# Padding rows of the expert slots written once the counts are known, and the first tokens' transposes moved to other PSUM banks

## The chip, the cores and the metric

One core of one Trainium2 chip runs the whole program. The metric is device microseconds (us) from the start to the end of one execution, lower is better. The notation of the rows: PE is TensorE's matmuls, DVE is VectorE, ACT is ScalarE, POOL is GpSimd, SP is SyncE, which here issues most of the DMAs; a "q" behind an engine's name is its sequencer (SPq), and L151 is line 151 of the kernel before.

## The reference

An mLSTM attention feeds a mixture of experts, and this a three-way maximum layer. What matters here is the middle part: a token with a positive skip score goes to one of eight experts, the others pass through.

```python
def _moe_ref(x, w_skip, w_gate, w1, w2):
    do_compute = x @ w_skip > 0
    out = x.copy()
    xc = x[do_compute]
    logits = xc @ w_gate
    e_idx = np.argmax(logits, axis=1)
    ...
    for e in range(E):
        mask = e_idx == e
        h = np.maximum(xc[mask] @ w1[e], 0.0)
        y[mask] = gate_w[mask, None] * (h @ w2[e])
    out[do_compute] = xc + y
    return out

def _moe2_ref(x, w1, w2, w3, w_out):
    h = np.maximum(np.maximum(x @ w1, x @ w2), x @ w3)
    return h @ w_out
```

There are 3072 tokens of 320 numbers, 8 experts with a hidden size of 1024, and a hidden size of 768 in the last layer.

## The kernel before

**Stages.** `attention` runs over 24 tiles of 128 tokens (index i in its long loop). For each it loads TP, KP and small rows (SA, SM), scores (`score`, L900), weighs, and puts the tokens' output with their routing numbers into a row of 323 words, which an indirect DMA on GpSimd scatters into a table in DRAM (`scatter`, L1118). Beside it the weights of the last layer are loaded by ScalarE's queue (mraw, L210) and split into a high and a low half for float32r matmuls. The table has eight sections of slots, one for each expert, and behind them one row for every token by its place. A tile of an expert's tokens is 128 slots; slots behind the expert's last token must hold rows whose index lies out of range, so that what is computed from them is written nowhere. Such a row is `zrow` (its index words are set in `consts`). `pads` (L777, its DMA at L781) writes 256 of them into the first slots of one section, in iterations 0 to 7, before any token is scattered.

**The seam.** When all tokens are routed, `counted` (L352 and following) works out with small VectorE operations which expert stands at which place of the order, how many tokens each has, and some addresses, all in one integer tile `cnt_i`. The generator `experts` then runs up to its first `yield`: it reads the eight experts' numbers into SP's registers (`ids`, L145), issues the first two weights (`load`, L151), the first expert's x (`xload`, L456: tiles 0 and 1 as one DMA, then tile 2 by itself), and three weights more. The first expert in the order is the largest and may have three tiles; its third tile is not covered by `pads`, so `xload` reads an address from `cnt_i` into a register and writes 128 rows of `zrow` behind the tokens (L453, L454), and tile 2 is loaded after that.

During this, TensorE works on the first of the last layer's blocks of 512 tokens that need no expert (`mixed_block`, called by attention as `early["run"]`, driven by `fill`). Its six hidden blocks end with two pairs of output groups: the first pair in the banks "row" (ic and pv), the second in "tr" (mi and pl). Between the pairs stands `xprep(0, j)` for j = 0 and 1, the transposes of the first expert's x (`x_parts`, L278 and L279), also in "tr". ScalarE and VectorE evacuate these (xT, L280 to L283).

**The experts' weights.** There are 64 of them, 384 KB for a slab of the first layer, 320 KB for one of the second. A raw weight is loaded into one of five buffers (RAWS), then ScalarE casts it (L160) and VectorE or GpSimd makes the low half (L161); the split weights stand in a ring of twelve. `step` splits the next and issues one more load, in program order between the matmuls. The first expert's four first-layer slabs are split while attention's mixed block runs; its four second-layer slabs are weights 5 to 8. In a slab s, `l1` (L471, into bank pd) and `few1` (L404 and L410, into ps) are followed by two splits, so ScalarE's queue holds hH and r of the slab, sH of the slab before, and the two casts, in this order.

**Order and waits.** All engines run in order, and the program's order is the order of the calls. Accesses to the table are tracked as a whole where addresses come from registers; `Ctx.apart` tells the scheduler for which groups of DMAs no order is needed ("slots" for the scatters, "xl" for the loads of x, "y" for the results, "pad" and "last" for the third tile). The DMAs of SP and ACT signal their landing on eight semaphores (DMAHW0 to DMAHW7), which are handed round, so a DMA also waits for the one eight before it.

Of the kernel before, what the change touches and what calls it, by code (L numbers as in the profile page):

```python
# [12 lines left out]
I32 = mybir.dt.int32  # L13
AF = mybir.ActivationFunctionType
ALU = mybir.AluOpType
# [6 lines left out]
N = B * S  # L22
DM = H * D
E, FF = 8, 1024
F2 = 768
D1 = D + 1
CAP = N + 128
RW = DM + 3
# [4 lines left out]
ST = 256  # L33
# [6 lines left out]
TILES = (3, 2, 1, 2, 1, 2, 1, 2)  # L40
# [11 lines left out]
def bc(ap, shape):  # L52
    return ap.to_broadcast(shape)


def build(tc, tp, kp, og, gates, w9, w1, w2, m1, m2, out):
    nc = tc.nc
    with ExitStack() as top:
        top.enter_context(tc.manual_schedule())
        cp = top.enter_context(tc.tile_pool(name="const", bufs=1))  # L60
        dram = top.enter_context(tc.tile_pool(name="dram", bufs=1, space=bass.MemoryType.DRAM))
        table = dram.tile([ROWS, RW], F32, name="table")
        rows = dram.tile([NC, 3, 2, B * H, NB], BF16, name="rows")

        k = Ctx()
        k.tc, k.nc, k.cp, k.out = tc, nc, cp, out
        k.table, k.rows = table, rows
        k.psum = top.enter_context(tc.tile_pool(name="psum", bufs=1, space=PSUM))
        k.ident = cp.tile([128, 128], F32, name="ident")

        k.zrow = cp.tile([128, RW], F32, name="zrow")

        k.cnt_i = cp.tile([1, 3 * E + 3], I32, name="cnt_i")

        k.ordr = cp.tile([1, E], F32, name="ordr")
        k.caps = cp.tile([1, E], F32, name="caps")

        mp = Mixed(k, top, m1, m2)  # L80
        wts = Weights(k, w1, w2)
        with ExitStack() as left:
            moe = experts(k, wts, mp, left)
            attention(k, tp, kp, og, gates, w9, wts, left, mp, lambda: next(moe))
            next(moe, None)
            final(k, mp, wts)
        rare(k, mp, wts)
# [264 lines left out]
def counted(k):  # L352

    nc, cn, ci = k.nc, k.cn, k.cnt_i
    v = nc.vector
    f8 = k.cp.tile([1, 5, E], F32, name="f8")
    f88 = k.cp.tile([1, 2, E, E], F32, name="f88")
    m1 = k.cp.tile([1, 4], F32, name="m1")
    own, rank, ids, n = (f8[:, j] for j in range(4))
    em = k.em8[0:1, 0:E]  # L360
    across = lambda x: bc(x.unsqueeze(1), [1, E, E])
    down = lambda x: bc(x.unsqueeze(2), [1, E, E])

    v.scalar_tensor_tensor(own, cn[:, 0:E], float(E), em, ALU.mult, ALU.subtract)
    v.tensor_tensor(f88[:, 0], across(own), down(own), ALU.is_gt)
    v.tensor_reduce(rank, f88[:, 0], AX.X, ALU.add)
    v.tensor_scalar(rank, rank, float(-E), None, ALU.add)

    v.tensor_tensor(f88[:, 0], across(rank), down(k.ordr), ALU.is_equal)
    v.tensor_mul(f88[:, 1], f88[:, 0], across(em))  # L370
    v.tensor_reduce(ids, f88[:, 1], AX.X, ALU.add)
    v.tensor_scalar(ids, ids, float(E), None, ALU.add)
    v.tensor_copy(ci[:, 0:E], ids)
    v.tensor_mul(f88[:, 1], f88[:, 0], across(cn[:, 0:E]))
    v.tensor_reduce(n, f88[:, 1], AX.X, ALU.add)
    v.tensor_copy(ci[:, E : 2 * E], n)
    v.scalar_tensor_tensor(f8[:, 4], ids, float(CAP), n, ALU.mult, ALU.add)
    v.tensor_copy(ci[:, 2 * E : 3 * E], f8[:, 4])

    z = ORDER.index(0)  # L380
    v.tensor_scalar(m1[:, 0:1], n[:, z : z + 1], float(ST), None, ALU.max)
    v.scalar_tensor_tensor(m1[:, 0:1], ids[:, z : z + 1], float(CAP), m1[:, 0:1], ALU.mult, ALU.add)
    v.tensor_copy(ci[:, 3 * E : 3 * E + 1], m1[:, 0:1])

    v.tensor_sub(n, n, k.caps)
    v.tensor_reduce(m1[:, 1:2], n, AX.X, ALU.max)
    v.tensor_copy(ci[:, 3 * E + 1 : 3 * E + 2], m1[:, 1:2])

    v.tensor_scalar(m1[:, 2:3], cn[:, E : E + 1], -1.0, float(EARLY), ALU.mult, ALU.add)
    v.tensor_scalar(m1[:, 3:4], cn[:, E + 1 : E + 2], -1.0, float(T2), ALU.mult, ALU.add)  # L390
    v.tensor_max(m1[:, 2:3], m1[:, 2:3], m1[:, 3:4])

    v.tensor_max(m1[:, 2:3], m1[:, 2:3], m1[:, 1:2])
    v.tensor_scalar(m1[:, 2:3], m1[:, 2:3], 0.0, None, ALU.max)
    v.tensor_copy(ci[:, 3 * E + 2 : 3 * E + 3], m1[:, 2:3])


def few1(k, wts, p2, hp, e, s, xt):
# [18 lines left out]
def l2(k, wts, p2, e, hs, c, xrow, apart=True):  # L417

    nc = k.nc
# [9 lines left out]
    y = wts.y.tile([128, RW], F32, tag="y", name="y", bufs=3)  # L429
# [3 lines left out]
        k.table, bass.IndirectOffsetOnAxis(ap=xrow.bitcast(I32)[:, PLC : PLC + 1], axis=0), y, None,  # L433
        bounds_check=ROWS - 1, oob_is_err=False)
    if apart:
        k.apart(ins, "y", "y", "xl", "last", "pad")


def experts(k, wts, mp, left):
    tc, nc = k.tc, k.nc  # L440
    X, XT = {}, {}
    p2 = wts.x
    sp = [mybir.EngineType.SP]

    def xload(e):

        own = k.table[0 : E * CAP].rearrange("(e c) r -> e c r", c=CAP)[bass.ds(wts.at[e], 1)]
        X[e] = []
        for j, n in ((0, min(TILES[e], 2)), (2, 1))[0 : 1 + (TILES[e] > 2)]:
            t = p2.tile([128, n, RW], F32, tag="xb" if n > 1 else "xc", name="xb")  # L450
            rows = own[:, 128 * j : 128 * (j + n)].rearrange("o (j p) r -> p (o j) r", p=128)
            if j:
                free = nc.values_load(k.cnt_i[0:1, 3 * E : 3 * E + 1], engines=sp, min_val=0, max_val=E * CAP - 128)  # L453
                k.apart(nc.sync.dma_start(k.table[bass.ds(free, 128)], k.zrow), "pad", "y", "xl")  # L454

            k.apart(nc.sync.dma_start(t, rows), *(("last", "y") if j else ("xl", "y", "pad")))  # L456
            X[e] += [t[:, q] for q in range(n)]

    def xprep(e, j):

        if j % 2 == 0:
            n = 128 * min(TILES[e] - j, 2)
            XT[e, j // 2] = planes(*(p2.tile([128, a, n], F32R, tag=f"x{n}{a}", name="xT", bufs=1) for a in (3, 2)))
        x_parts(k, X[e][j], XT[e, j // 2], slice(128 * (j % 2), 128 * (j % 2) + 128))

    def l1(e, s, xt):

# [9 lines left out]

    counted(k)
    wts.ids(sp)
    wts.ahead(2)  # L480
    xload(0)
    wts.ahead(RAWS - 2)
    yield
    for j in range(2):
        xprep(0, j)
    yield
    own = ExitStack()
    wts.more(own)
# [90 lines left out]
def rare(k, mp, wts):  # L579


    tc, nc = k.tc, k.nc
    some = nc.values_load(k.cnt_i[0:1, 3 * E + 2 : 3 * E + 3], min_val=0, max_val=N)
    with tc.If(some > 0), ExitStack() as own:
        wts.open(own)
        wts.more(own)
# [39 lines left out]
            return wts.y.tile([128, RW], F32, tag="y", name="o", bufs=3)[:, 0:DM]  # L626

        hl = []
        left = nc.values_load(k.cnt_i[0:1, 3 * E + 1 : 3 * E + 2], min_val=-N, max_val=N)
        with tc.If(left > 0):  # L630
            for e in range(E):
                more(e)
# [8 lines left out]
def attention(k, tp, kp, og, gates, w9, wts, left, mp, moe):  # L641
    tc, nc = k.tc, k.nc
    rows, table, ident, zrow = k.rows, k.table, k.ident, k.zrow
    with ExitStack() as ctx:
# [128 lines left out]
        def w9split():  # L773
            nc.scalar.copy(w18[:, :, 0], w9s)
            nc.vector.tensor_sub(w18[:, :, 1], w9s, w18[:, :, 0].bitcast(F32))

        def pads(e):  # L777


            r0, n = e * CAP, ST  # L780
            nc.sync.dma_start(table[r0 : r0 + n, :].rearrange("(j p) r -> p j r", p=128),  # L781
                              bc(zrow.unsqueeze(1), [128, n // 128, RW]))

        gt = {}

# [435 lines left out]
        for i in range(NT):  # L1221
# [10 lines left out]
                w9load()  # L1232
            if i == 3:
                w9split()
            if i < E:
                pads(i)
            if i == NT - 4:
                early_load()
            rts = [todo.pop() if todo else None, rts[0]]
# [155 lines left out]
```

## Time and profile before

| what | us |
|---|---|
| median of 3 runs | 587.95 |
| lowest and highest | 586.24, 590.15 |
| the profiled execution | 588.96 |
| its span on the core | 587.2 |
| TensorE's matmuls busy | 547.4 (93%) |
| VectorE busy | 314.1 (53%) |
| ScalarE busy | 235.6 (40%) |
| GpSimd busy | 229.0 (39%) |

The span is what the trace covers; 1.76 us of the profiled execution lie around it. Attention takes the first third, the experts run from about 234 to 347 us, the last layer follows. The granted clock of TensorE was 0.976 of full on the mean. A busy share is an average over stages with different limits, so the sections below go by stage.

### The profile page before, as it was taken

What the parts mean: (1) busy time and instruction counts of PE and PEld (TensorE: products, weight loads), DVE (VectorE), ACT (ScalarE), POOL (GpSimd) and SP (SyncE); (2) the same over time, 40 slices, a digit from 0 to 9 for tenths busy, and PEclk for the clock granted to TensorE, in tenths of its full rate; (3) what the DMA queues carried; (4) which work ended last, traced back from release to release, by engine and by line L of the source; (5) the groups of instructions that cost most, each with busy time, mean ns of one, the idle gap of its engine ahead of it and who ended that gap; (6) DMA issues with size and microseconds to landing.
All of it is one profiled execution on the core that took longest, in us unless ns stands there. A gap on an engine that the chain in (4) does not pass through costs nothing.

```text
span 587.2 us, 10688 instructions
## 1 busy us (share of the span) xinstructions
PE 547.4 (93%) x3890; PEld 478.1 (81%) x3890; DVE 314.1 (53%) x786; ACT 235.6 (40%) x505; POOL 229.0 (39%) x271
## 2 busy tenths in 40 slices
PE   7978988989979998999999999999999999999990
PEld 4866777777868778999999988898898898898890
DVE  7768989998866673677787532312212311311210
ACT  5554645554622333768677422221222222222120
POOL 4325667687754442242424412131231232132231
PEclk9989988999979999999999999999999999999996
DMA  6687877687740137569887511010001001000000
GB/s 224 179 284 229 285 232 221 221 271 226 237 150 23 47 110 249 171 196 308 250 284 251 157 56 55 0 46 1 1 35 56 1 33 58 1 24 23 0 25 27
DMA packets 38631, 77.01 MB, mean 131 GB/s; under 512 B 6446, under 2 KB 20783, under 8 KB 38568
## 3 DMA queue, kind: packets, MB, share of 16 engines
q1 hardware_dynamic: 27528, 57.33, 30.9%
q10 hardware_dynamic: 8064, 9.05, 5.1%
q0 software_dynamic: 2976, 9.85, 4.4%
q8 instruction: 33, 0.54, 0.4%
q14 instruction: 30, 0.25, 0.1%
HBM read 63.30 MB, written 13.27 MB: 130 GB/s over the span
## 4 chain that ended last, share of the span: by engine, by line
PE 71%; DVE 11%; DMA 7%; issue 3%; POOL 3%; ACT 2%; SPq 0%; ACTq 0%; POOLq 0%; DVEq 0%
PE pd L322 17%; PE ps L322 17%; PE pd L471 6%; PE pv L965 3%; PE ps L404 3%; DMA mraw<-m 2%; DMA SA<-rows 2%; DMA TP<-tp 2%; PE pv L426 1%; PE pv L428 1%; PE ic L427 1%; PE ic L428 1%; PE ic L426 1%; PE pv L427 1%; PE ps L900 1%
## 5 line engine op out<-in xcount | busy, mean ns | idle before, releaser
L303 POOL TENSOR_TENSOR hL<-t,hH 128x512 fp32r<-128x512 f32 x30 | 38.6, 1288 | 141.5 <-ACT hH L302 141.5
L161 DVE TENSOR_TENSOR w<-raw,w 128x768 fp32r<-128x768 f32 (+1 forms) x48 | 48.5, 1037 | 14.3 <-ACT w L160 14.3
L965 PE MATMUL pv<-KP,W 128*128 128x123 f32 (+2 forms) x384 | 55.2, 290 | 0.1
L302 ACT CAST hH<-t 128x512 fp32r<-128x512 f32 x30 | 18.6, 621 | 90.5 <-DVE t L312 90.5
L160 ACT CAST w<-raw 128x768 fp32r<-128x768 f32 (+1 forms) x64 | 49.2, 786 | 13.3 <-DMA raw<-w 8.2
L965 PEld LDWEIGHTS pv<-KP,W 128*128 128x128 f32 x384 | 49.8, 200 | 3.4 <-DVE xs L972 0.4
L311 DVE TENSOR_TENSOR t<-t,ps 128x512 f32<-128x512 f32 x15 | 10.3, 688 | 64.3 <-PE ps L322 64.2
L322 PE MATMUL ps<-fxH,mH 128*128 128x512 f32 x108 | 43.3, 401 | 0.0
L322 PE MATMUL pd<-fxH,mH 128*128 128x512 f32 x108 | 43.0, 399 | 0.0
L322 PE MATMUL ps<-fxH,mL 128*128 128x512 f32 x108 | 42.8, 396 | 0.0
L322 PE MATMUL pd<-fxH,mL 128*128 128x512 f32 x108 | 42.8, 396 | 0.0
L985 POOL TENSOR_TENSOR g<-O,den 128x320 f32<-128x320 f32 x24 | 19.9, 829 | 58.1 <-DVE den L982 36.0
L891 ACT ACTIVATE W<-pd 128x512 f32<-128x512 f32 x48 | 27.9, 592 | 27.5 <-PE pd L890 21.3
L471 PE MATMUL pd<-xT,w 128*128 128x256 f32 x288 | 37.8, 283 | 0.0
L900 PE MATMUL ps<-TP 64*128 64x128 f32 x384 | 30.7, 301 | 6.5 <-DMA TP<-tp 4.3
L471 PEld LDWEIGHTS pd<-xT,w 128*128 128x128 f32 x288 | 35.4, 188 | 0.2 <-DVE hL L475 0.2
L900 PEld LDWEIGHTS ps<-TP 64*128 64x128 f32 x384 | 25.8, 201 | 11.0 <-DVE den L982 3.0
L432 POOL DMA_INDIRECT table<-y,xb x14 | 14.3, 1023 | 52.2 <-DMA raw<-w 13.5
L161 POOL TENSOR_TENSOR w<-raw,w 128x640 fp32r<-128x640 f32 x16 | 25.2, 1580 | 20.1 <-ACT w L160 20.0
L908 DVE TENSOR_TENSOR W<-ps,W 128x512 f32<-128x512 f32 x48 | 30.5, 675 | 1.4 <-PE ps L900 1.0
L344 POOL DMA_INDIRECT out<-o,fx x20 | 19.6, 982 | 28.4 <-ACT o L343 26.9
L1118 POOL DMA_INDIRECT table<-XR,si x24 | 24.6, 1023 | 11.6 <-DVE xi L946 5.2
(376 smaller groups left out, 1498.0 us busy)
## 6 DMA issues: line engine op xcount, KB each, us to landing
TP<-tp SPq DMA_DIRECT2D x24, 512.0 KB
raw<-w SPq DMA_DIRECT2D x32, 384.0 KB
raw<-w SPq DMA_DIRECT2D x32, 320.0 KB
KP<-kp SPq DMA_DIRECT2D x24, 324.0 KB
mraw<-m ACTq DMA_DIRECT2D x18, 384.0 KB
O<-og SPq DMA_DIRECT2D x6, 640.0 KB
fx<-table SPq DMA_DIRECT2D x5, 642.0 KB
table<-zrow SPq DMA_DIRECT2D x8, 323.0 KB
```

The source lines that it names most:

```text
L160: nc.scalar.copy(hi, r)
L161: (nc.gpsimd if m and s % 2 else nc.vector).tensor_sub(lo, r, hi.bitcast(F32))
L303: nc.gpsimd.tensor_sub(g, t, h.bitcast(F32))
L322: nc.tensor.matmul(p, w, z, start=i == 0, stop=i == len(tt) - 1)
L344: ins = nc.gpsimd.indirect_dma_start(k.out, bass.IndirectOffsetOnAxis(ap=x.bitcast(I32)[:, j + q, IDC : IDC + 1], axis=0), o, None, bounds ...
L471: nc.tensor.matmul(ps[:, f], w, x, start=f == 0 and i == 0, stop=f == 1 and i == 7)
L891: nc.scalar.activation(st[i]["W"][:, q], pd, AF.Exp)
L900: nc.tensor.matmul(ps[q][:, j], TP[r, 1, j], TP[r, 0, j], start=True, stop=True)
L908: nc.vector.tensor_mul(t["W"][:, q], t["ps"][q], t["W"][:, q])
L965: nc.tensor.matmul(t["pv"][:, h:h1], t["W"][:, h % 2, h // 2], t["ve"][:, h:h1], start=True, stop=True)
L985: nc.gpsimd.tensor_mul(g, sg[c][:, b], bc(den.unsqueeze(2), [128, H, D]))
L1118: ins = nc.gpsimd.indirect_dma_start(table, bass.IndirectOffsetOnAxis(ap=si, axis=0), x, None, bounds_check=ROWS - 1, oob_is_err=False)
```

## The change

The eight DMAs of `pads` in attention's loop are gone. In their place `experts` has a `pads(e)` that writes, for each of the expert's tiles j, 128 rows of `zrow` from an address that comes from the counts: behind the tokens for j = 0, behind the larger of the tokens and 128 for j = 1, and of the tokens and 256 for j = 2. That makes 14 DMAs of 161.5 KB, each behind a register load: three for the first expert before the first weights, eleven for the others behind the fifth weight. `counted` works out eight more addresses with three operations. `xload` no longer writes a pad. The transposes of the first expert's tiles 0 and 1 go into the banks "acc" (pd and ps).

```diff
@@ build
-        k.cnt_i = cp.tile([1, 3 * E + 3], I32, name="cnt_i")
+        k.cnt_i = cp.tile([1, 4 * E + 3], I32, name="cnt_i")
@@ counted
     v.tensor_copy(ci[:, 2 * E : 3 * E], f8[:, 4])
+    v.tensor_scalar(f8[:, 4], n, 128.0, None, ALU.max)
+    v.scalar_tensor_tensor(f8[:, 4], ids, float(CAP), f8[:, 4], ALU.mult, ALU.add)
+    v.tensor_copy(ci[:, 3 * E : 4 * E], f8[:, 4])
...
-    v.tensor_copy(ci[:, 3 * E : 3 * E + 1], m1[:, 0:1])
+    v.tensor_copy(ci[:, 4 * E : 4 * E + 1], m1[:, 0:1])
...
@@ l2
     if apart:
-        k.apart(ins, "y", "y", "xl", "last", "pad")
+        k.apart(ins, "y", "y", "xl", "pad")
@@ experts
+    def pads(e):
+
+        for j in range(TILES[e]):
+            at = 4 * E if j == 2 else (2 + j) * E + e
+            free = nc.values_load(k.cnt_i[0:1, at : at + 1], engines=sp, min_val=0, max_val=E * CAP - 128)
+            k.apart(nc.sync.dma_start(k.table[bass.ds(free, 128)], k.zrow), "pad", "slots", "xl")
+
     def xload(e):
...
-            if j:
-                free = nc.values_load(k.cnt_i[0:1, 3 * E : 3 * E + 1], engines=sp, min_val=0, max_val=E * CAP - 128)
-                k.apart(nc.sync.dma_start(k.table[bass.ds(free, 128)], k.zrow), "pad", "y", "xl")
-
-            k.apart(nc.sync.dma_start(t, rows), *(("last", "y") if j else ("xl", "y", "pad")))
+            k.apart(nc.sync.dma_start(t, rows), "xl", "y")
...
-    def xprep(e, j):
+    def xprep(e, j, bank="tr"):
...
-        x_parts(k, X[e][j], XT[e, j // 2], slice(128 * (j % 2), 128 * (j % 2) + 128))
+        x_parts(k, X[e][j], XT[e, j // 2], slice(128 * (j % 2), 128 * (j % 2) + 128), bank)
...
     wts.ids(sp)
+    pads(0)
     wts.ahead(2)
     xload(0)
     wts.ahead(RAWS - 2)
+    for e in range(1, E):
+        pads(e)
     yield
     for j in range(2):
-        xprep(0, j)
+        xprep(0, j, "acc")
@@ attention
-        def pads(e):
-
-
-            r0, n = e * CAP, ST
-            nc.sync.dma_start(table[r0 : r0 + n, :].rearrange("(j p) r -> p j r", p=128),
-                              bc(zrow.unsqueeze(1), [128, n // 128, RW]))
...
-            if i < E:
-                pads(i)
```

In `rare` only the places in `cnt_i` change.

On SP's queue, at the seam, the fifth weight's load is followed at once by the sixth and seventh in the program before (raw is a weight's buffer, in brackets what the row waits for; ISA rows set registers).

```order
L151 DMA raw<-w 128x640 [waits DMAHW3_49]
L151 ISA
L151 DMA raw<-w 128x640 [waits DMAHW4_49,DVE_49]
L151 ISA
L151 DMA raw<-w 128x640 [waits DMAHW5_49,DVE_49]
```

In the changed program eleven pads stand between the fifth and the sixth weight; these are the last three of them (table<-zrow) and the sixth weight. The three signal on DMAHW6, DMAHW7 and DMAHW0.

```order
L454 DMA table<-zrow 128x323 [waits DMAHW5_49]
L453 TENSOR_LOAD cnt_i
L453 ISA x2
L454 ISA
L454 DMA table<-zrow 128x323 [waits DMAHW6_49]
L453 TENSOR_LOAD cnt_i
L453 ISA x2
L454 ISA
L454 DMA table<-zrow 128x323 [waits DMAHW7_49]
L152 ISA
L152 DMA raw<-w 128x640 [waits DVE_49]
```

Each pad waits for the semaphore on which the pad before it signals; the weight behind them waits for none of them, but stands behind their issue.

On TensorE, between the two pairs of output groups of attention's mixed block, the transposes of x (ident, xb) stand in the same place in both programs. Before, they and the group behind them use the banks mi and pl:

```order
L339 MATMUL pv<-oH,eh 128x320
L278 MATMUL mi<-ident,xb 128x128 [waits DMAHW6_49,PE_49]
L278 MATMUL mi<-ident,xb 128x128
L279 MATMUL mi<-ident,xb 64x128
L278 MATMUL pl<-ident,xb 128x128 x2
L279 MATMUL pl<-ident,xb 64x128
L337 MATMUL mi<-oH,eh 128x320 [waits DVE_49,PE_49]
```

In the changed program the transposes go to pd and ps (all lines of `x_parts` and `mixed_block` are one higher):

```order
L340 MATMUL pv<-oH,eh 128x320
L279 MATMUL pd<-ident,xb 128x128 [waits DMAHW1_49,DVE_49]
L279 MATMUL pd<-ident,xb 128x128
L280 MATMUL pd<-ident,xb 64x128
L279 MATMUL ps<-ident,xb 128x128 x2
L280 MATMUL ps<-ident,xb 64x128
L338 MATMUL mi<-oH,eh 128x320 [waits PE_49]
```

The wait for VectorE ahead of the output group in mi is no longer there; nothing else on TensorE moves.

## Rows read from the trace of the kernel before

**Rows 1.** The page, part 1: busy us, share and count.

```profile
PE 547.4 (93%) x3890; PEld 478.1 (81%) x3890; DVE 314.1 (53%) x786; ACT 235.6 (40%) x505; POOL 229.0 (39%) x271
```

**Rows 2.** The chain in order of time, 0 to 60 us: start, us, what.

```profile
0.84 2.33 DMA G<-gates
...
26.81 5.93 DMA TP<-tp
32.87 1.82 PE ps L900 x16
...
47.84 1.80 DMA SM<-rows
```

**Rows 3.** TensorE's waits, 14 to 60 us: total us, times, longest.

```profile
PE ps L900 <- DMA TP<-tp: 3.8, 2, 2.8
...
PE pd L890 <- DMA SM<-rows: 0.7, 1, 0.7
```

**Rows 4.** Windows: PE, PEld, DVE, ACT, POOL busy; PEclk, DMA share, GB/s.

```profile
34.00:42.00 8.00, 8.00 (x90) 6.86 (x88) 3.20 (x7) 4.42 (x6) 2.45 (x3) 0.84 0.83 241
...
216.00:228.00 12.00, 10.70 (x63) 9.53 (x61) 6.21 (x8) 6.46 (x13) 3.96 (x4) 1.00 0.80 268
...
236.00:246.00 10.00, 10.00 (x87) 10.00 (x86) 5.96 (x9) 8.03 (x15) 3.17 (x2) 1.00 0.53 153
```

**Rows 5.** Timeline of SP's DMA issues, 213 to 240 us: start, us, what.

```profile
213.53 0.93 SPq L151 DMA_DIRECT2D raw<-w  x2
214.79 0.38 SPq L456 DMA_DIRECT2D xb<-table  x1
215.98 0.38 SPq L454 DMA_DIRECT2D table<-zrow  x1
219.74 0.34 SPq L456 DMA_DIRECT2D xb<-table  x1
220.27 7.88 SPq L151 DMA_DIRECT2D raw<-w  x7
```

**Rows 6.** TensorE's waits, 206 to 300 us.

```profile
PE mi L337 <- DVE xT L283: 1.9, 1, 1.9
```

**Rows 7.** VectorE's timeline, 210 to 224 us; in brackets idle before, and releaser.

```profile
210.59 0.16 DVE L378 CAST cnt_i<-f 1x8 int32<-1x8 f32 x1
...
212.37 0.69 DVE L311 TENSOR_TENSOR et<-et,pd 128x512 f32<-128x512 f32 x1
...
220.83 0.69 DVE L312 TENSOR_TENSOR et<-et,ps 128x512 f32<-128x512 f32 x1 [0.89 <-PE ps L322]
221.44 0.95 DVE L161 TENSOR_TENSOR w<-raw,w 128x768 fp32r<-128x768 f32 x1
```

**Rows 8.** ScalarE's timeline, 216 to 241 us.

```profile
217.06 0.83 ACT L160 CAST w<-raw 128x768 fp32r<-128x768 f32 x1
...
221.55 0.62 ACT L302 CAST eh<-et 128x512 fp32r<-128x512 f32 x1 [2.31 <-DVE et L312]
223.22 0.83 ACT L160 CAST w<-raw 128x768 fp32r<-128x768 f32 x1 [1.04 <-DMA raw<-w]
...
237.56 1.34 ACT L160 CAST w<-raw 128x640 fp32r<-128x640 f32 x2
239.19 0.60 ACT L474 ACTIVATE hH<-pd 128x512 fp32r<-128x512 f32 x1 [0.28 <-PE pd L471]
240.14 0.39 ACT L406 ACTIVATE r<-ps 128x256 f32<-128x256 f32 x1 [0.35 <-PE ps L404]
240.42 0.37 ACT L412 CAST sH<-ps 128x256 fp32r<-128x256 f32 x1
```

**Rows 9.** GpSimd's timeline, 222 us: the low half of the last hidden block.

```profile
222.25 1.31 POOL L303 TENSOR_TENSOR eh<-et,eh 128x512 fp32r<-128x512 f32 x1 [3.72 <-ACT eh L302]
```

**Rows 10.** TensorE's timeline, 225 to 243 us.

```profile
225.29 0.31 PE L339 MATMUL ic<-oH,eh 128*128 128x320 f32 x1
...
242.06 1.11 PE L404 MATMUL ps<-w,xT 128*128 128x256 f32 x8
```

More of the change, by code (lines that the diff above doesn't have):

```diff
@@ L382, in counted @@
     v.scalar_tensor_tensor(m1[:, 0:1], ids[:, z : z + 1], float(CAP), m1[:, 0:1], ALU.mult, ALU.add)
-    v.tensor_copy(ci[:, 3 * E : 3 * E + 1], m1[:, 0:1])
+    v.tensor_copy(ci[:, 4 * E : 4 * E + 1], m1[:, 0:1])
     v.tensor_sub(n, n, k.caps)
     v.tensor_reduce(m1[:, 1:2], n, AX.X, ALU.max)
-    v.tensor_copy(ci[:, 3 * E + 1 : 3 * E + 2], m1[:, 1:2])
+    v.tensor_copy(ci[:, 4 * E + 1 : 4 * E + 2], m1[:, 1:2])
     v.tensor_scalar(m1[:, 2:3], cn[:, E : E + 1], -1.0, float(EARLY), ALU.mult, ALU.add)
@@ L394, in counted @@
     v.tensor_scalar(m1[:, 2:3], m1[:, 2:3], 0.0, None, ALU.max)
-    v.tensor_copy(ci[:, 3 * E + 2 : 3 * E + 3], m1[:, 2:3])
+    v.tensor_copy(ci[:, 4 * E + 2 : 4 * E + 3], m1[:, 2:3])
 def few1(k, wts, p2, hp, e, s, xt):
@@ L582, in rare @@
     tc, nc = k.tc, k.nc
-    some = nc.values_load(k.cnt_i[0:1, 3 * E + 2 : 3 * E + 3], min_val=0, max_val=N)
+    some = nc.values_load(k.cnt_i[0:1, 4 * E + 2 : 4 * E + 3], min_val=0, max_val=N)
     with tc.If(some > 0), ExitStack() as own:
@@ L628, in rare @@
         hl = []
-        left = nc.values_load(k.cnt_i[0:1, 3 * E + 1 : 3 * E + 2], min_val=-N, max_val=N)
+        left = nc.values_load(k.cnt_i[0:1, 4 * E + 1 : 4 * E + 2], min_val=-N, max_val=N)
         with tc.If(left > 0):
```

## The prediction

> **What bounds the kernel now.** The page comes first: TensorE is busy for 547.4 of 587.2 us [rows 1], so the time is TensorE's own work plus the places where it waits, and an edit counts only where it opens or shuts such a place. The chain that ended last, read in order of time, shows where waits other than TensorE's own come in: in the first 60 us it runs through transfers, for instance 5.93 us on the load of TP that ends just before a score group starts at 32.87 [rows 2]. The chain alone says too much, since TensorE works beside most of these transfers. The list of waits says what it lost: 3.8 us for TP and 0.7 us for SM between 14 and 60 us [rows 3]. The windows add that its granted clock was 0.84 of full on the mean of the 8 us from 34 on [rows 4], which follow the longest of these waits (2.8 us).
>
> The change's second place is the seam between attention and the first expert, 213 to 243 us. There I read SP's timeline, which is nothing but DMA issues: two weights at 213.53, the first tokens' x at 214.79, one padding write ("pad" below) at 215.98, the third x tile at 219.74 after that pad had landed, then seven weights from 220.27 on [rows 5]. TensorE waits once here, 1.9 us, for the evacuation of the transposed x (xT) [rows 6]. From 236 to 246 us, in the first expert, TensorE is full [rows 4], so what is lost there is not given back.
>
> **The change part by part.** The sum is made against the profiled execution's own 588.96 us (span 587.2 and 1.76 around it), which is 1.0 above the median of 587.95; the gain or loss is then put on the median.
>
> *Eight pads go from the first eight tiles of attention.* Each moves 256 rows of 323 words, 323 KB; 2.65 MB in all. What this can give back to TensorE is bounded below by nothing and above, by its waits, by 3.8 + 0.7 = 4.5 us [rows 3] and the slow clock: a mean of 0.84 over 8 us is 2.6 us at the lower of its two levels (1.2 GHz, the rest at 2.4), which is 1.3 us of work lost [rows 4]; together 5.8. A bound by bytes lies higher: 2.65 MB at the 241 GB/s of that window is 11.0 us. The pad stands ahead of the TP load on SP's queue and both share the engines, so I take off most of the waits but not all, as TP's 512 KB stay: -4.5 us. On this the Trainium skill, in "DMA: Bandwidth & Descriptors", section "Issuing engines are not separate DMA queues", says that all queues share the same 16 DMA engines; taken to its end, every byte removed relieves every transfer, and the sum would go by the bytes. The trace bears that out only in part, since the transfers on the chain are several times as long as the waits; it is rival D.
>
> *Three operations more in the count.* VectorE's L378 and its neighbours take 0.16 us and follow each other without idle time, and behind them stands the maximum that TensorE's next group waits for [rows 7]. That is 3 x 0.16 = +0.5 us, 0 if VectorE's place were not on the path.
>
> *Three pads ahead of the first weights.* One pad costs SP 0.81 us for the register load before its issue (from 214.79 + 0.38 to 215.98) [rows 5]. The order of the changed program adds what the diff does not show: a pad waits for the pad before it, semaphore by semaphore, because pads are told to be apart from "slots" and "xl" but not from "pad". So a step from pad to pad is a full landing, not an issue. What does a landing cost? 2.33 us for 32 KB with nothing ahead, 1.80 for 3 KB [rows 2], 2.95 from issue to use for 384 KB (220.27 to 223.22) [rows 5, 8], and 3.76 for the one pad here, which stood behind an x load and two weights (215.98 to 219.74) [rows 5]. A pad of 161.5 KB that stands alone lies between 2.33 and 2.95; I take 2.4, nearer to the small one, and keep 1.80 and 3.76 as ends. Then pads are issued at 214.1, 216.5 and 218.9, the first weight at 219.5 instead of 213.53, and it lands at 222.4. ScalarE's queue holds its cast ahead of work for the last hidden block of attention's mixed block: cast 0.83, VectorE's low half 0.95, two maxima of 0.69, ScalarE's cast of eh 0.62, GpSimd's low half 1.31 [rows 7 to 9] end at 227.5, while TensorE wants this at 225.29 + 0.5 = 225.8 [rows 10]. That is +1.7 us, 0 where the weight lands 1.7 us sooner, and at most the weight's own lateness, 5.4 us.
>
> *Transposes in other banks.* The wait of 1.9 us goes, since the output groups behind the transposes no longer need the banks that these fill [rows 6]: -1.9 us. What is late next is x itself (xb waits for the third pad at 221.3 and lands behind two weights) and the first expert's weights; xb is there by 226 at the latest, so I keep the whole 1.9.
>
> *Eleven pads ahead of the sixth weight.* From 220.5 on, 2340 KB stand in the queue (five weights and x), 8.9 us at 268 GB/s [rows 4], to 229.4. The first late pad is issued near 224 and lands behind them, near 230.6. The other ten are each issued when the one before has landed: the last at 230.6 + 9 x 2.4 = 252.2. The sixth weight, before the fourth of the seven issues from 220.27, follows at 252.8 and lands 2.95 later, at 255.7. ScalarE wants it as the second of the pair at 237.56, that is at 238.2 [rows 8]. Its queue is in order: behind this cast stand hH (0.60), r (0.39) and sH (0.37), and sH frees the bank that TensorE's group at 242.06 needs [rows 8, 10]. So TensorE goes on until 242.06 + 0.3 and starts again at 255.7 + 0.7 + 0.6 + 0.4 + 0.4 + 0.2 = 258.0: +15.6 us. With landings of 1.80 it is 10.2, with 3.76 it is 27.8. Little hides this: the sixth weight's cover is that its issue stood, near 222, some 16 us ahead of a cast for which 3 would do; the eleven pads take 30. Behind it, weights 7 to 16 come in a row; the second layer of the first expert needs only weights 5 to 8, so I add nothing for the others.
>
> The row on a pad is the 3.76 us above, not freed of its queue. The Trainium skill ("DMA: Bandwidth & Descriptors", section "Anatomy of one DMA — SWDGE (gpsimd) path") says that most of a transfer's fixed cost is the receipt of the write, and that the wait can be long above all when the target is HBM, as a pad's is. By that rule the pad's step is not a load's but nearer to 3.76, and the sum +25.3; no row here shows a pad alone, and it is rival C.
>
> *The clock after the stall.* The wait of 2.8 us was followed by a clock of 0.84 for 8 us, 1.3 us lost [rows 3, 4]; I take somewhat more for fifteen: +1.7, between 0 and 4.
>
> Sum: -4.5 + 0.5 + 1.7 - 1.9 + 15.6 + 1.7 = +13.1 us, 602.1 for a profiled execution and 601.0 on the median.
>
> **Rivals.** A is the forecast.
>
> B, a gain: the pads hold nobody, as in a program where they did not wait for each other. Then each costs its issue, 215.98 - 214.79 = 1.19 us: the first weight lands at 220.1 and the 1.7 us in the mixed block are gone; ten more issues from 224.2 put the sixth weight at 236.7, and it lands at 239.7. TensorE, 1.4 us early by now, wants its group at 240.7 and gets it at 242.0, +1.3. The sum is -4.5 + 0.5 - 1.9 + 1.3 = -4.6, 583.4. The point from which it decides: with A's other terms at +0.3 - 4.5 + 1.7, the stall may be 2.5 us, so the nine steps 8.5 in place of 21.6, 0.95 us each; above that the change is slower. For it speaks that the one pad before is a single short issue in SP's timeline; against it the semaphores in the order, and that no transfer in the rows landed in less than 1.80.
>
> C, slower still: each late pad takes the 3.76 us of the row. Nine steps of 1.36 more are +12.2: 613.2. For it speaks that this is the only pad whose end a row shows; against it that it stood behind 1.1 MB.
>
> D, no change: the early stretch gives by bytes, -11.0 instead of -4.5, and steps are 1.80, -5.4: +13.1 - 6.5 - 5.4 = +1.2, 589.2. Against it: TensorE waited only 4.5 us in all there.
>
> **How the numbers follow.** A 0.70, B 0.08, C 0.13, D 0.09. The range, 591 to 613, leaves out B, the half of C that lies above its price and the low half of D. A measurement of this kernel can tell about 1% (5.9 us) from no change. Slower by more than that is nearly all of A and C, 0.83. Within it lie D and half of B, 0.13. Faster is left with 0.04, the half of B in which the early stretch gives more than 4.5 us.
>
> **What would show it.** Right: on SP eleven pads some 2.4 us apart, each after a wait for a pad; the sixth weight issued near 250 (less what the early stretch gave); one TensorE wait of 12 to 18 us between the first expert's second and third slab, with the chain running through the pads; no wait at the outputs that follow the transposes; TP waits of TensorE under 2 us in the first 60. Wrong: pads issued about 1.2 us apart and TensorE full from 236 on (B); a gain of over 7 us before 80 us (D).

## The result and the profile after

The changed kernel took 596.32 us, the median of four runs (594.01 to 598.17), beside 587.10 of the kernel before on the same chip: a ratio of 1.0147, 95% interval 1.011 to 1.0185, or 8.6 us more. Differences in us between kernels are taken from such ratios here and below. Timed once more on another chip it stood 11.7 us over before. 601.0 was predicted, within 591 to 613. The profiled execution of after took 597.86 us; its span is 596.1.

From the profile's page of after: its part 1 (busy time), its part 4 (shares of the chain that ended last), and two groups of its part 5:

```profile
PE 547.7 (92%) x3890; PEld 478.5 (80%) x3890; DVE 314.4 (53%) x789; ACT 235.2 (39%) x505; POOL 229.4 (38%) x271
...
PE ps L323 16%; PE pd L323 16%; DMA table<-zrow 5%; PE pd L478 5%; PE pv L968 3%; PE ps L408 2%; DVE mtmp L240 2%; DVE mtmp L227 1%; DVE xTL L1008 1%; PE ic L430 1%; PE pv L430 1%; PE pv L432 1%; PE ic L431 1%; PE ic L432 1%; PE pv L431 1%
...
L161 ACT CAST w<-raw 128x768 fp32r<-128x768 f32 (+1 forms) x64 | 48.9, 787 | 33.5 <-DMA raw<-w 30.6
...
L408 PE MATMUL ps<-w,xT 128*128 128x256 f32 x128 | 18.8, 292 | 13.6 <-DVE sL L417 13.6
```

TensorE's busy time is what it was [rows 1], over a longer span. What is new stands in two places: the padding writes (table<-zrow) hold 5% of the chain, and one group of the first expert, L408, has idle time of 13.6 us ahead of it. ScalarE's casts of the weights wait 30.6 us for loads.

TensorE's waits of after from 200 to 320 us (us in total, times, longest):

```profile
PE ps L408 <- DVE sL L417: 13.6, 1, 13.6
PE ic L338 <- ACT eh L303: 1.6, 1, 1.6
PE ic L340 <- POOL eh L304: 0.8, 1, 0.8
PE pd L323 <- DVE et L312: 0.7, 1, 0.7
```

[rows 6] had one wait of 1.9 us at the outputs, which is gone. Where it comes from is in the chain of after in order of time (start, us, what), from the seam to the group that waited:

```profile
208.25 2.00 DMA table<-zrow
210.27 1.94 DMA table<-zrow
212.22 2.65 DMA table<-zrow
...
218.33 6.05 DMA table<-zrow
224.40 2.13 DMA table<-zrow
226.65 1.97 DMA table<-zrow
...
242.48 1.93 DMA table<-zrow
244.43 0.33 SPq L454
244.96 3.55 DMA raw<-w
248.54 0.72 ACT w L161
249.26 0.51 ACT hH L481
249.79 0.57 DVE hL L482
250.40 0.42 DVE sL L417
250.87 2.07 PE ps L408 x8
```

Every piece named table<-zrow is a padding write ("pad") that the next one waits for; SyncE's own waits say the same, twelve waits of 15.6 us in sum:

```profile
SPq L454 <- DMA table<-zrow: 15.6, 12, 4.7
```

The first three stand ahead of the weights that [rows 5] issue at 213.53. The first of the eleven lands after 6.05 us, behind five weights; from 224.40 to 244.43 there are nine steps in 20.03 us, 2.23 each. Only then is the sixth weight issued, and the cast and the evacuations behind it on ScalarE and VectorE lead to TensorE. No piece of the chain between 208.25 and 250.87 is TensorE's.

The windows of after, for the stall and what follows it (us; PE, PEld, DVE, ACT, POOL busy; PEclk, DMA share, GB/s):

```profile
237.25:250.87 13.62, 0.00 (x1) 0.01 (x1) 1.02 (x2) 2.33 (x6) 1.47 (x1) 0.63 0.47 154
250.87:254.50 3.63, 3.63 (x17) 3.63 (x18) 1.94 (x3) 2.65 (x7) 1.63 (x2) 0.50 1.02 379
254.50:260.00 5.50, 5.50 (x43) 5.50 (x43) 4.65 (x6) 4.47 (x10) 0.00 (x0) 1.00 0.77 260
```

TensorE stands still for 13.62 us, and its granted clock is then 0.50 (the 1.2 GHz level) for 3.6 us: 1.8 us of work lost on top.

In attention, the counts mark how early the stretch ended. This row of VectorE's timeline of after

```profile
201.59 0.16 DVE L374 CAST cnt_i<-f 1x8 int32<-1x8 f32 x1
...
206.56 0.69 DVE L312 TENSOR_TENSOR et<-et,pd 128x512 f32<-128x512 f32 x1
```

answers to this one of the kernel before, where the maximum behind the counts starts at 212.37 [rows 7]:

```profile
207.98 0.16 DVE L373 CAST cnt_i<-f 1x8 int32<-1x8 f32 x1
```

The counts come 6.4 us earlier, and from this cast to the maximum it is 4.97 us instead of 4.39: the three added operations cost 0.6. Of the TP waits of 3.8 us [rows 3] one is left between 14 and 60 us; another wait, behind VectorE, is longer than in before (1.5 us, there 0.6):

```profile
PE mi L851 <- DVE R L845: 1.5, 1, 1.5
PE ps L903 <- DMA TP<-tp: 0.7, 1, 0.7
```

### The profile page after: what moved, and what is told of

The parts are those of the page before. It is cut to its first block, busy times and chain, and to the rows that moved or that the text cites. A ratio compares the mean times of both kernels' runs of the same rounds, so it can differ in the third digit from the quotient of the medians.

```text
span 596.1 us, 10757 instructions
## 1 busy us (share of the span) xinstructions
PE 547.7 (92%) x3890; PEld 478.5 (80%) x3890; DVE 314.4 (53%) x789; ACT 235.2 (39%) x505; POOL 229.4 (38%) x271
## 4 chain that ended last, share of the span: by engine, by line
PE 65%; DVE 14%; DMA 8%; POOL 4%; issue 4%; ACT 2%; SPq 1%; ACTq 0%; POOLq 0%
PE ps L323 16%; PE pd L323 16%; DMA table<-zrow 5%; PE pd L478 5%; PE pv L968 3%; PE ps L408 2%; DVE mtmp L240 2%; DVE mtmp L227 1%; DVE xTL L1008 1%; PE ic L430 1%; PE pv L430 1%; PE pv L432 1%; PE ic L431 1%; PE ic L432 1%; PE pv L431 1%
## 5 line engine op out<-in xcount | busy, mean ns | idle before, releaser
L161 ACT CAST w<-raw 128x768 fp32r<-128x768 f32 (+1 forms) x64 | 48.9, 787 | 33.5 <-DMA raw<-w 30.6
L408 PE MATMUL ps<-w,xT 128*128 128x256 f32 x128 | 18.8, 292 | 13.6 <-DVE sL L417 13.6
## 6 DMA issues: line engine op xcount, KB each, us to landing
table<-zrow SPq DMA_DIRECT2D x14, 161.5 KB
```

The costliest lines, as they stand in the source:

```text
L161: nc.scalar.copy(hi, r)
L408: nc.tensor.matmul(ps, x[:, 0:128], w, start=i == 0, stop=i == len(tt) - 1)
```

## Experiments

The theory: the late pads stall TensorE because each waits for the landing of the one before, on the queue that brings the weights. Rivals were the bytes of the pads, and a cost of each write by itself. None of these kernels leaves part of the computation out. Taking the chain away while each tile keeps its own write was not tried, since two writes of one expert can cover the same rows; so the chain is taken away below from eight writes, not from fourteen.

**One write for each expert, chained as before.**

```diff
-        for j in range(TILES[e]):
-            at = 4 * E if j == 2 else (2 + j) * E + e
-            free = nc.values_load(k.cnt_i[0:1, at : at + 1], engines=sp, min_val=0, max_val=E * CAP - 128)
-            k.apart(nc.sync.dma_start(k.table[bass.ds(free, 128)], k.zrow), "pad", "slots", "xl")
+        n = TILES[e]
+        at = 2 * E + e
+        free = nc.values_load(k.cnt_i[0:1, at : at + 1], engines=sp, min_val=0, max_val=E * CAP - 128 * n)
+        k.apart(nc.sync.dma_start(k.table[bass.ds(free, 128 * n)].rearrange("(j p) r -> p j r", p=128),
+                                  bc(k.zrow.unsqueeze(1), [128, n, RW])), "pad", "slots", "xl")
```

> The changed kernel, but each expert gets one padding write of 128 rows per tile behind its tokens: one write instead of three ahead of the first weights, seven instead of eleven ahead of the sixth weight, each still waiting for the one before, the bytes the same. Theory (a chain of landings): a step costs 2.2 us, and at most 0.6 us more where it writes 161.5 KB more; the late steps take 15.6 to 18.1 us instead of 24.5, TensorE's wait for the first expert's third weight slab falls from 13.6 to between 5 and 9.5 us, and the three first steps of 6.2 us become one of 2.2 to 3.4 us; the time is 587 to 592 us. Rival (bytes on the queue): the bytes are as before, so the wait stays near 13.6 us and the time at 595 to 597 us.

588.25 us, 1.0039 of before (1.0012 to 1.0067). TensorE's wait is 7.5 us instead of 13.6, and the waits at L338 and L340 are gone. The chain of this kernel measures a step for two sizes, as the late pads alternate between 323 KB (two tiles) and 161.5 KB:

```profile
219.77 6.83 DMA table<-zrow
226.62 2.42 DMA table<-zrow
229.05 2.85 DMA table<-zrow
231.93 2.14 DMA table<-zrow
234.19 2.72 DMA table<-zrow
236.93 2.35 DMA table<-zrow
```

The first, 6.83, waited behind the weights, as in after. Then 161.5 KB took 2.42, 2.14 and 2.35 (mean 2.30), 323 KB 2.85 and 2.72 (mean 2.79): twice the bytes cost 0.5 us more, so, as an estimate from these two means, some 1.8 us of a step do not depend on the bytes. The bytes' rival falls: the bytes are as before, and the time lies in the theory's range.

**The same without the chain.** Writes of different experts never meet, so they may be told to be apart from each other.

```diff
-                                  bc(k.zrow.unsqueeze(1), [128, n, RW])), "pad", "slots", "xl")
+                                  bc(k.zrow.unsqueeze(1), [128, n, RW])), "pad", "slots", "xl", "pad")
```

> As the kernel with one write for each expert, but the padding writes do not wait for one another; the count of writes and the bytes stay. Theory (a chain of landings): the seven late writes are issued within a microsecond or so each, the sixth weight is issued before 228 instead of at 245 us, TensorE's wait of 13.6 us and the half clock behind it are gone, and the time is before's 587.1 with the early gain (4.5 to 6.3), the banks (1.9) and the longer counting (+0.5): 579 to 583 us. Rival (each padding write holds the queue 2.2 us by itself, waited for or not): seven of them still delay the sixth weight by about 15 us, a wait of 5 to 9 us stays, and the time is 586 to 592 us.

582.48 us, 0.9951 of before (0.9916 to 0.9986). By the ratio that is 584.2 where before is at 587.1, 1.2 above the theory's range and below the rival's. In SP's timeline the seven late writes and the four weights behind them are

```profile
213.79 8.26 SPq L454 DMA_DIRECT2D table<-zrow  x7
222.32 2.11 SPq L152 DMA_DIRECT2D raw<-w  x4
```

that is 1.2 us for each write with its register load, and the sixth weight at 222.32 instead of 244.96. The wait of 13.6 us is gone. One of 2.2 us is new. Here are the line of TensorE's waits, and the row of ScalarE's timeline that it points to (in brackets the idle time before, and its releaser):

```profile
PE mi L279 <- ACT eo L344: 2.2, 1, 2.2
```

```profile
225.41 0.42 ACT L344 COPY eo<-mi 128x320 f32<-128x320 f32 x1 [5.43 <-DMA out<-eo,ex]
```

The window around it and the one behind it, columns as above:

```profile
220.00:226.00 6.00, 3.85 (x27) 3.59 (x26) 1.12 (x4) 0.42 (x1) 0.89 (x1) 1.00 1.00 280
226.56:229.97 3.41, 3.41 (x18) 3.41 (x18) 0.71 (x2) 0.73 (x4) 1.51 (x2) 0.50 0.97 345
```

ScalarE waited 5.43 us for writes of outputs to land, and the window says that the DMA engines were busy all of the 6 us (share 1.00). Behind the wait TensorE's clock was at its lower level for 3.41 us, 1.7 us of work lost. So the bytes do cost something once they come in a burst: 3.9 us here, against 15.4 in after. This is the only kernel below whose interval lies wholly under before. Its gain lies in attention: from the counts' cast to the first long group of the last layer (199.18 to 341.93) its profiled execution takes 142.75 us, that of before (207.98 to 347.44) 139.46.

**More of the same: the late pads twice.**

```diff
-    for e in range(1, E):
+    for e in [*range(1, E), *range(1, E)]:
         pads(e)
```

> The changed kernel with the eleven late padding writes issued twice, 22 steps instead of 11 ahead of the sixth weight; the output is unchanged. Theory (a chain of landings, 2.23 us a step): TensorE's wait for the third weight slab grows from 13.6 by 11 x 2.23 = 24.5 us to about 38 us, and the time to 619 to 624 us (the clock may fall once more). Rival (the bytes decide): 1.78 MB more at 268 GB/s are 6.6 us, the time is 601 to 604 us. Rival (a step costs 1.19 us, the rest of the wait is something else): 13 us more, 608 to 611 us.

624.25 us, 1.0619 of before (1.058 to 1.0658), and the wait is

```profile
PE ps L408 <- DVE sL L417: 38.2, 1, 38.2
```

24.6 us more than in after for eleven more pads: 2.24 us each. The steps do not change when there are twice as many, and TensorE has no further cover: each step comes through in full. The time lies at the upper end of the theory's range (623.4 by the ratio where before is at 587.1), far above both rivals'.

**The banks alone**, in the kernel before.

```diff
-        x_parts(k, X[e][j], XT[e, j // 2], slice(128 * (j % 2), 128 * (j % 2) + 128))
+        x_parts(k, X[e][j], XT[e, j // 2], slice(128 * (j % 2), 128 * (j % 2) + 128), bank)
...
-        xprep(0, j)
+        xprep(0, j, "acc")
```

> The kernel before with only the banks of the first tokens' transposes changed. Theory: TensorE's wait of 1.9 us at the first output group behind the transposes is gone and the time is 1.5 to 2.2 us lower, 585 to 585.6 us. Rival (a wait on another engine's read takes its place): no change, 586.5 to 587.5 us.

584.77 us, 0.9977 of before (0.9945 to 1.0009). In its trace TensorE has no wait of 0.3 us or more between 206 and 300 us, where [rows 6] had 1.9. The time fell by 1.3 us by the ratio, which the interval does not tell from nothing; that the wait went and that none took its place is shown by the one profiled execution.

**The early writes kept as well.**

```diff
+            if i < E:
+                early_pads(i)
```

(early_pads is the old function of attention, with its write of 256 rows.)

> The changed kernel, and the eight early padding writes of 323 or more KB are kept in attention's first iterations as well (written twice, the output is unchanged). Theory (the early writes hold attention's first iterations): the time goes up by 4.5 to 6.3 us, to 600.5 to 603 us, and TensorE's waits for the transposes of the first iterations come back to 3 to 5 us in sum. Rival (the early gain in the two profiles is where the clock happened to fall): 595.5 to 597.5 us.

602.90 us, 1.0287 of before (1.0226 to 1.0349): 16.8 us over before, against 8.6 and 11.7 for after. The counts' cast stands at 205.87, where after had 201.59. The waits of the score group came back (between 14 and 60 us):

```profile
PE ps L908 <- DVE mtmp L227: 3.2, 1, 3.2
PE ps L908 <- DMA TP<-tp: 1.2, 1, 1.2
PE ps L908 <- DVE mtmp L240: 0.9, 1, 0.9
```

The profile puts two of them down to VectorE's mtmp, but these matmuls neither read nor write mtmp. They wait for two semaphores, VectorE's, which moves every few tenths of a us, and that of the load of TP; the profile names the one that moved last. At the end of the wait of 3.2 us the load's moved at 47.572 us and VectorE's at 47.579, at the end of that of 0.9 at 32.049 and 32.092. So all three are read as waits for TP, 5.3 us in sum. Counted in the same way, the score groups of the three executions with writes of 323 KB (before, banks alone, this one) wait 3.8, 2.9 and 5.3 us there; in the eight without early writes it is never more than 1.3.

**Early writes of one row**, 1.3 KB instead of 323, in the same eight iterations; then all eight in the fifth iteration.

```diff
+        def early_pads(e):
+            nc.sync.dma_start(table[e * CAP : e * CAP + 1, :], zrow[0:1, :])
...
+            if i < E:
+                early_pads(i)
```

> The changed kernel and, in attention's first eight iterations, one write of a single row of 1.3 KB where the kernel before wrote 256 rows. Theory (the early writes cost by their bytes): the early gain stays, the time is 595.5 to 598 us. Rival (they cost by their place in the queue and their issue): most of the 6.6 us that writing them in full brought back comes back, 600 to 603 us.

602.12 us, 1.0249 (1.0204 to 1.0294), 14.6 us over before, in the rival's range: by this time alone the place of a write would cost as much as its bytes.

```diff
-            if i < E:
-                early_pads(i)
+            if i == 4:
+                for e in range(E):
+                    early_pads(e)
```

> The changed kernel with the eight one-row writes of attention's first eight iterations issued all together, in the fifth iteration. Eight semaphores are shared in turn by the DMAs of the hardware queues, so that each DMA waits for the eighth before it; eight writes in one place shift that turn by nothing for all that follows. Theory (what costs is that each write shifts the turn, so that loads wait for another load's landing): most of the gain comes back, 596 to 599 us. Rival (what costs is the issue of each write on SyncE's queue): the same eight issues, 600 to 604 us.

602.43 us, 1.0293 (1.024 to 1.0346), 17.2 us over before and in the rival's range. But its profiled execution, 599.63 us, has the counts' cast at 201.23, as early as a kernel without early writes, and a longer stall of 14.9 us: the median and the trace disagree. These kernels had been timed on other chips than after, so after and the first of the two were run once more, side by side.

> The changed kernel once more, on the chip of the run beside it, since the three kernels with early writes were timed on other chips than it was. Its time stands 8.6 us over before in its first four runs; theory: 8 to 10 us again, 595.5 to 597.5 us where before is at 587. Rival (its first four runs were low by chance, and the early gain is smaller than 6 us): 11 to 13 us over before, 598 to 600 us.

> The changed kernel with a write of one row in each of attention's first eight iterations, once more. Theory (the place of a write in the queue costs, not its bytes): 4.5 to 6.5 us over the changed kernel beside it. Rival (it is the bytes, and the earlier run stood high by its chip): within 1.5 us of the changed kernel beside it.

After: 599.79 us beside 588.58 of before, 1.0198 (1.0154 to 1.0242). With one-row writes: 600.99 us, 1.0243 (1.0196 to 1.029). By the first, what was expected of after falls to its rival: over both series it stands 8.6 to 11.7 us above before. The one-row writes stand 2.6 us higher beside it (the medians 1.2), which lies between theory and rival, with intervals that overlap; in all three runs of theirs they are above both series of after. That they cost something is likely; how much, and by which path, is not settled. It is not the path of the old writes: the score groups wait 0, 1.0 and 0 us between 14 and 60 us in the three profiled executions with one-row writes.

The counts' cast in the profiled executions tells the sizes better, as it excludes all that comes later. With the old early writes (before, banks alone, early writes kept) it stands at 207.98, 207.64 and 205.87, mean 207.2. Without (after twice and the six other kernels without early writes) it lies between 199.18 and 205.42, mean 202.4. With one-row writes it stands at 206.77, 201.23 and 202.07. So the writes that went had cost 4.8 us on the mean, and no execution of the one kind reaches into the other, if only by 0.45 us. The three with one row lie on both sides of this; the waits for TP that came back with 323 KB and not with one row speak for the bytes.

The spread of the eight without early writes goes with TensorE's granted clock. From 13 us to the cast its mean was 0.97 in the two earliest (199.18 and 200.47), 0.96 in the next four, and 0.95 in the two latest (204.68 and 205.42).

**Padding by unit.** The first expert's pads behind the first two weights, the others ahead of each unit's token loads; first with one chained write for each tile, then with one unchained write for each expert.

```diff
-    pads(0)
     wts.ahead(2)
+    pads(0)
     xload(0)
     wts.ahead(RAWS - 2)
-    for e in range(1, E):
-        pads(e)
...
+            for e in UNITS[n + 1]:
+                pads(e)
             for e in UNITS[n + 1]:
                 xload(e)
```

(In these kernels the pads are told to be apart from "y" as well, so that they don't wait for the scatters of finished tokens.)

> The changed kernel, but the padding of the first expert is written behind the first two weights' loads, and that of each later expert just before its tokens are loaded, a unit ahead of use; still one write for each tile, each waiting for the one before. Theory: two to three steps of 2.2 us a unit find room in the weights' lead there; no wait of TensorE over 3 us is left between the experts' slabs, and the time is before's with the early gain (5 to 6.6 us), the banks (1.5 to 1.9) and the counting (+0.5): 578 to 582 us. Rival (the steps hold the weights in every unit in which they stand): 4 units by 4 to 7 us come on top, 590 to 605 us.

601.35 us, 1.0246 (1.0213 to 1.028): the rival's range. TensorE waits five times for 1.7 to 4.0 us, 14.6 us in sum, all at L279, the transposes of tokens (xb).

> As the kernel with the padding by unit, with one write for each expert, none waiting for another. Theory: the writes no longer stand between weights and outputs in one burst, so the output group's wait of 2.2 us that the kernel without the chain had is gone too: 576.5 to 581 us, 1 to 3 us below that kernel. Rival (the outputs' wait comes from elsewhere): as that kernel, 581 to 583.5 us.

592.32 us, 1.0096 (1.0068 to 1.0124): above the rival's range too. The wait of 2.2 us at the outputs did go, but two new ones stand in its place. Here are TensorE's waits, 240 to 340 us, the windows of each wait and of what follows it, and what SyncE waited for in the whole execution:

```profile
PE pl L279 <- issue: 3.8, 1, 3.8
PE mi L279 <- issue: 3.0, 1, 3.0
```

```profile
270.19:273.19 3.00, 0.01 (x1) 0.04 (x1) 2.96 (x7) 2.69 (x8) 0.99 (x1) 0.82 0.90 286
273.19:278.92 5.73, 5.73 (x22) 5.69 (x23) 4.45 (x8) 3.93 (x8) 0.98 (x1) 0.50 0.85 283
299.82:303.63 3.81, 0.00 (x2) 0.03 (x1) 3.77 (x8) 3.70 (x10) 0.99 (x1) 0.89 0.79 224
303.63:309.64 6.01, 6.01 (x24) 5.97 (x25) 4.45 (x8) 3.72 (x8) 0.98 (x1) 0.50 0.91 313
```

```profile
SPq L464 <- DMA table<-zrow: 18.2, 5, 3.9
```

The token loads (L464) wait for the pads just ahead of them, and that holds everything behind them on SyncE's queue. The tokens themselves came in time: their loads were issued at 262.57 and 263.24 and had landed by 265.9, and TensorE's wait begins at 270.19. Late were the weights behind them, as in after. ScalarE's cast waits for one, and the evacuation of the transposes before (xT), which frees the bank mi, stands behind such casts and their low halves on ScalarE and VectorE:

```profile
268.06 0.83 ACT L161 CAST w<-raw 128x768 fp32r<-128x768 f32 x1 [4.54 <-DMA raw<-w]
```

```profile
272.80 0.28 DVE L284 TENSOR_TENSOR xT<-mi,xT 64x128 fp32r<-64x128 f32 x1
```

TensorE goes on at 273.18, when this has ended. The second wait runs the same way: a cast waits 4.58 us for a weight, and the evacuation that frees pl is the last work ahead of TensorE.

The two waits are 6.8 us in sum, and behind them TensorE works at half clock for 5.7 and 6.0 us, 5.9 us of work lost in both together: 12.7 us. The kernel without the chain lost 3.9 to its burst, so 8.8 us more are expected here; by the ratios it is 8.5 (on different chips).

**The same, a unit earlier.**

```diff
+    for e in UNITS[1]:
+        pads(e)
     yield
...
-            for e in UNITS[n + 1]:
-                pads(e)
             for e in UNITS[n + 1]:
                 xload(e)
+            for e in UNITS[n + 2] if n + 2 < len(UNITS) else ():
+                pads(e)
```

> As the kernel with the padding by unit and one write for each expert, but each write is issued a unit earlier, behind the loads of the tokens of the unit before. Theory (in the run before, the tokens' loads waited for padding written just ahead of them, 3.0 and 3.8 us before the transposes and about as much of half clock behind each): these two waits go, and the time is 578 to 583 us, at or below the kernel without the chain. Rival (any padding write between the weights' loads costs its place there, wherever it stands): 588 to 593 us as before.

586.00 us, 0.9978 (0.995 to 1.0006): the two waits are down to 1.1 and 0.7 us, as the theory has it, but the time lies between its range and the rival's. From the counts' cast to the last layer the profiled execution takes 141.90 us (204.68 to 346.58), 0.9 less than the kernel that writes the pads in one burst without a chain; its cast comes 5.5 us later, in attention, where the code of the two is the same. The intervals of the two times overlap, so which is better is not told.

## Why the prediction was right

The forecast was a slower kernel by a chain of landings ahead of the sixth weight, and that is what the runs show: take the chain away and the loss becomes a small gain; double it and the stall grows step by step. The size was 601.0 against 596.3, and 599.8 in the second series. By its terms:

- *Early pads gone, -4.5.* The profiled executions of before and after differ by 6.4 us at the counts, the mean over all kernels is 4.8. The term was right within what one execution varies, and a gain by all the bytes (-11.0) is excluded. Its reason, TP's waits, holds: the score groups wait 2.9 to 5.3 us with these writes and 0 to 1.3 without.
- *Three operations in the count, +0.5.* 0.6 measured.
- *Three pads ahead of the first weights, +1.7.* The waits at L338 and L340, 1.6 + 0.8 = 2.4 us in after, at the block and by the path that were named; with one write instead of three they are gone.
- *Banks, -1.9.* The wait went, in after and alone.
- *Eleven pads ahead of the sixth weight, +15.6.* 13.6 measured: the term that was mis-sized, by 2.0. TensorE goes on 49.3 us behind the counts' cast, where the prediction had 50.0; a step is 2.23 us instead of 2.4, 1.6 less over nine, and the landing of the weight 3.55 instead of 2.95 takes part of that back. The other 1.3 is TensorE's own: it reaches the group 35.7 us behind the cast, where the prediction had 34.4. The order of events was as worked out, but for the last link (VectorE's sL frees the bank, not ScalarE's sH); the weight's landing and TensorE's restart are 2.4 us apart against 2.3.
- *The clock, +1.7.* 1.8 measured. The row that the term was made from begins 0.8 us after the clock had fallen (it was 0.50 from 33.20 to 36.61 in before), so the wait of 2.8 us had cost 1.7 and not 1.3. The reason given, somewhat more for the longer stall, does not show: behind stalls of 12.4 to 15.1 us in the six executions with this chain 1.5 to 2.6 us were lost, behind the 38.2 us of the doubled one 3.1, and behind waits of 3.0 and 3.8 us 2.9 and 3.0.

One thing the sum left out. The stall ends when the chain ends, whatever TensorE did before: in the six executions with eleven late pads TensorE goes on 49.3 to 50.6 us behind the counts' cast, while its stall is 12.4 to 15.1 us. So the operations in the count, the waits in the mixed block and the banks only move the start of the stall; in after the banks buy no time. The prediction added these terms beside the stall and did not set them against it. They come to +0.3 there, so the sum did not suffer.

The terms as these two executions have them are -6.4 + 0.6 + 2.4 - 1.9 + 13.6 + 1.8 = +10.1 us. TensorE's last matmul stands 10.0 us later:

```profile
573.70 0.31 PE L339 MATMUL pl<-oH,hL 128*128 128x320 f32 x1
```

```profile
583.68 0.30 PE L340 MATMUL pl<-oH,hL 128*128 128x320 f32 x1
```

(the first of before, the second of after). The profiled times differ by 8.9, as what follows the last matmul was 1.1 us shorter in after. With the mean of 4.8 for the early pads the sum is +11.7 against the predicted +13.1. That it meets the second series, +11.7, is in part luck, since the first, +8.6, is the same kernel.

Rival B (1.19 us for a write that nobody waits for) describes the kernel without the chain: 1.2 us for each of its writes. So its price was right and its condition was missing: the semaphores decide. That 582.48 us lies near B's 583.4 is in part luck: this kernel has eight writes, not fourteen, and its burst cost 3.9 us, where B reckoned with a wait of 1.3. Rival C fell: the steps are 2.23 us. The 3.76 us of the one pad in before are read as its place behind weights, as the 6.05 of the first late pad in after. On this the Trainium skill ("DMA: Bandwidth & Descriptors", section "Anatomy of one DMA — SWDGE (gpsimd) path") gives a fixed part of 2.0 us and the bytes at 436 GB/s, which makes, as an estimate, 2.38 us for 161.5 KB and 2.76 for 323; the chain's 2.30 and 2.79 agree with it, though these writes were issued from SyncE. That a receipt from HBM can take surprisingly long, as the Trainium skill says in the same section, does not show in these steps. Rival D needed a gain by bytes of 11.0 us and fell with it.

## What to carry to other kernels

Writes to one tensor at addresses from registers wait for each other unless the scheduler is told that they are apart. A write that waits holds the queue for a landing (2.2 us here) instead of an issue (1.2 with its register load), and with it everything behind it on that queue; count such steps against the lead of the load that comes next. Fewer and larger writes help by their number, since doubling the bytes of one costs only 0.5 us. A write placed just ahead of a load of the same tensor makes that load wait, and the weights behind it: put it a unit earlier, or undo the chain and accept a short burst. And where a stall ends with a chain on another queue, work saved ahead of it only lengthens the stall.

## What was not expected

- A short wait can cost more than itself: behind TensorE waits of 3.0 and 3.8 us the granted clock was 0.50 for 5.7 and 6.0 us, behind one of 2.2 us (no chain) for 3.4, behind the stall of 13.6 for 3.6. It is not the wait's length alone: behind 1.9 us in before, and behind 2.2 at L338 in the second execution of after, it stayed at 1.00.
- Attention's length varies by 6 us between executions of kernels whose code there is the same (the counts' cast at 199.18 to 205.42). One pair of profiles gave 6.4 us for a term that is 4.8 on the mean, and four runs put the whole difference 3.1 us lower than six did.
- Kernels with a write of one row, 1.3 KB, in eight iterations stood 14.3 to 17.2 us over before, where after stood 8.6 and 11.7; by which path is open.
